# Splitting the low maxima on VectorE and moving one subtraction from TensorE to GpSimd in a sparse attention and mixture kernel

## The chip, the cores and the metric

The kernel runs on one core of one Trainium2 chip. The metric is the time of one launch in microseconds (us), the median of three runs. Five engines work side by side, each through its own list of instructions in order: TensorE (PE in the profile, its weight loads PEld), VectorE (DVE), ScalarE (ACT), GpSimd (POOL) and SyncE (SP, which here only issues transfers). An instruction that must wait for another engine holds up everything behind it on its own engine.

## The reference, cut to what matters

```python
def _attn_ref(q, k, v):                       # 8 batches, 8 heads, 576 rows, 64 columns
    scores = (1 / 8) * np.matmul(q, k.transpose(0, 1, 3, 2))
    kth = np.partition(scores, -32, axis=-1)[..., -32:-31]
    scores = np.where(scores >= kth, scores, -1000000000.0)
    ...                                       # softmax over what is left
    return np.matmul(attn, v)

def reference(...):
    x = attn_out.transpose(0, 2, 1, 3).reshape(8, 576, 512)
    return _moe_ref(x, ...)                   # 4 experts, each causal attention of 64 columns, the best 2 by gate
```

Each of the 8 x 8 x 576 rows of scores keeps its 32 largest. Then a softmax, the product with the values, and over the eight heads' results a mixture of four attention experts.

## The kernel before, in words

Two heads form a pair, so there are 32 pairs (8 batches of 4). A pair has nine tiles of 128 score rows, worked in three groups of three tiles; 96 groups in all. A pair goes through these stages:

- *Scores.* TensorE multiplies queries with keys (`scores`), ScalarE copies each tile of 128 x 576 scores from PSUM to SBUF (`copy`, L1070, tile `s`; two buffers of three tiles).
- *Top 32* (`topk`), the work of VectorE. `f1` (L1083) takes the larger and `f3` (L1086) the smaller of the two halves of 576, so 288 each, into `fa` and `fb`. `f4` is three tensor operations: A (L1090) the larger of the halves of `fa`, into `cand`; B (L1091) the smaller of them, written into `fa` itself; C (L1093) the larger of the halves of what A made, into `oct`. `low8` is three MAX8 (L1097), one for each tile, which find the eight largest of `fb`. Then `f5` (three MAX8 on B's result, L1110), and four rounds of `win` (MAX8, L1121) and `rep` (MATCH_REPLACE8, L1126). Meanwhile GpSimd does `mark` (L1102) and `low2` (L1106) on A's and C's results, `tails` (L1113) and `compare` (L1150, for the group before).
- *Stats and tail* (`stats`, `tail`). The scores are made a second time, transposed and masked (`st`), ScalarE takes the exponential (L1374, tile `pt`), and TensorE multiplies by the values `vt` into the single accumulator `acc` (`av`). The result is needed as a high part (rounded for TensorE's fast format) and the low part that the rounding left. `xh` (L1386) copies `acc` to the high part; TensorE then adds minus that high part to `acc` by a product with a negated identity (`neg`, two matmuls, 256 and 320 columns); `xl` (L1394) copies what is left. The values' buffer `vt` is single too: the load for the next pair (L968, issued from ScalarE's list) may start when `av` has read it.
- *Mixture* (`moe`), once in a batch, spread over the four pairs after it. The mixture of the last batch has no later pair to lie beside. For the last pair of all, `tail` runs in two halves (`half` is set).

GpSimd also makes low parts of the queries and keys in SBUF (`sub`, L924, two in each of 31 pairs), of the mixture's output (L1798) and of the weights (L861).

The order of every engine's list is fixed when the program is built. `Plan` takes tasks with a modelled duration, what they depend on and a priority; `order` simulates five engines and writes out the list. The table `AT` gives each task's priority by its tag; a task goes when it has the smallest number among those that could start within 150 ns of the earliest. Nothing of that simulation is used at run time, only the order that came out of it.

Of the kernel before, what the change touches and what calls it, by code (L numbers as in the profile page):

```python
# [102 lines left out]
class Plan:  # L103
# [5 lines left out]
    PORT = ("f1", "f3", "f4", "ot", "constants", "sub", "low_again")  # L109
# [32 lines left out]
    def __init__(self):  # L142
        self.tasks = []
        self.rings = set()
        self.due = 0.0
        self.at = {t: iter(x) for t, x in AT.items()}
        self.slack = 150.0

    def restart(self):
        self.tasks, self.at, self.slack = [], {}, self.SLACK  # L150
        for r in self.rings:
            r.free = [(0.0, f[1], "") for f in r.free]
# [19 lines left out]
    def order(self):  # L172
# [11 lines left out]

        def pick(e):
            free, cand = engs[e]
            feas = []
            for t, r in cand:
                s = max(free, r)
                if e == "POOL":  # L190
                    s = max(s, port["DVE"] + (0.0 if t.tag == "mark" else self.GAP))
                elif e == "DVE" and t.tag in self.PORT:
                    s = max(s, port["POOL"])
                need = {}
                for b in t.bufs:
                    if b.index is None:
                        k = need.get(b.ring, 0)
                        if k >= len(b.ring.free) or (b.ring.fifo and b.seq != b.ring.given + k):
                            break
                        need[b.ring] = k + 1  # L200
                        f = b.ring.free[k]
                        s = max(s, f[0] + self.hop(f[2], e))
                else:
                    feas.append((s, t.prio, t.n, t))
            if not feas:
                return None
            lim = min(x[0] for x in feas) + self.slack
            return min((x for x in feas if x[0] <= lim), key=lambda x: x[1:3])

        for t in self.tasks:  # L210
# [5 lines left out]
        while len(out) < len(self.tasks):  # L216
            for e in engs:
                if e in stale:
                    picks[e] = pick(e)
            best = min((x for x in picks.values() if x), key=lambda x: x[0], default=None)  # L220
# [54 lines left out]
def pool(n):  # L275
    return 2.15 * n + 165


def dma(n, rows=P):
# [8 lines left out]
PAD = {"dup1": 400.0, "dup2": 1200.0, "s10": 800.0, "s11": 300.0, "dup": 400.0, "diag": 300.0, "c7": 400.0,  # L288
# [23 lines left out]
    "again": (109, 131, 709, 670, 1023, 976, 1291, 1268, 1516, 1521, 1854, 1832, 2083, 2091, 2464, 2469, 2706, 2726,  # L312
# [7 lines left out]
    "ava": (10291,),  # L320
    "avb": (10424,),
    "avm": (2307, 2807, 3690, 4082, 4989, 5346, 6220, 6608, 7509, 7869, 8751, 9138, 9921, 10231, 10824, 10842, 10856,
        10903,),
    "c1": (2273, 2780, 3524, 3946, 4816, 5336, 6045, 6491, 7311, 7838, 8578, 9010, 9880, 10176, 10584, 10700, 10790,
        10833,),
    "c2": (2283, 2783, 3537, 3973, 4822, 5344, 6061, 6505, 7328, 7854, 8581, 9032, 9898, 10179, 10587, 10703, 10794,
        10837,),
    "c3": (2294, 2797, 3539, 3975, 4881, 5346, 6063, 6507, 7330, 7856, 8584, 9034, 9900, 10182, 10590, 10706, 10797,
        10844,),
    "c4": (2343, 2838, 3548, 3989, 4921, 5376, 6086, 6550, 7345, 7899, 8607, 9117, 9920, 10218, 10602, 10715, 10810,  # L330
        10854,),
    "c5": (2350, 2846, 3550, 4025, 4934, 5389, 6108, 6553, 7353, 7908, 8634, 9124, 9923, 10223, 10604, 10718, 10813,
        10856,),
    "c6": (2356, 2848, 3553, 4028, 4936, 5392, 6110, 6555, 7355, 7910, 8652, 9135, 9927, 10225, 10607, 10722, 10817,
        10860,),
    "c7": (2377, 2871, 3575, 4050, 4958, 5418, 6146, 6576, 7378, 7940, 8675, 9157, 9959, 10247, 10629, 10743, 10838,
        10882,),
    "cast": (38, 73, 178, 167, 405, 685, 854, 1000, 1140, 1274, 1426, 1519, 1651, 1837, 1964, 2114, 2258, 2481, 2634,
# [1632 lines left out]
```

## Time and profile before

| what | value |
|---|---|
| runs | 1138.55, 1139.99, 1141.31 us; median 1139.99 us |
| profiled execution | 1139.88 us; its span from first to last instruction 1138.1 us |
| TensorE busy | 1052.2 us, 92% of the span |
| VectorE busy | 1023.4 us, 90% |
| ScalarE busy | 931.4 us, 82% |
| GpSimd busy | 408.6 us, 36% |
| granted TensorE clock, mean | 0.971 of full |

The profiled execution is one more run, 0.11 us below the median of the three, and 1.8 us of its time lies outside its span. A busy share is an average over stages. A matmul's recorded duration overlaps that of its neighbours, so a busy TensorE is not one at its peak.

### The profile page before, as it was taken

The page shows a single profiled execution, that of the slowest core. Times are in us where ns is not written, and L with a number is a line of the kernel's source. Part 1 is how long each engine was busy: PE and PEld are TensorE (multiplying, and loading weights), DVE is VectorE, ACT ScalarE, POOL GpSimd, SP SyncE. Part 2 cuts the span into 40 slices and gives each one's busy share as a digit, 9 for nine tenths or more (in the row PEclk, how much of TensorE's full clock was granted, in tenths as well). Part 3 has the DMA queues.
Part 4 walks back from the last instruction along what each step waited for, and adds up shares of the span by engine and source line. Part 5 has one row for each costly group of instructions (what it writes and reads, how often), then busy time and mean ns, then how long its engine had stood idle before and what let it go on. Part 6 is the DMA issues. An engine that isn't in the chain of part 4 may idle for free. (4 is left out here: it accounts for less than half of the span.)

```text
span 1138.1 us, 27832 instructions
## 1 busy us (share of the span) xinstructions
PE 1052.2 (92%) x9101; PEld 882.2 (78%) x9101; DVE 1023.4 (90%) x4231; ACT 931.4 (82%) x1966; POOL 408.6 (36%) x696
## 2 busy tenths in 40 slices
PE   3378799999999999999999999999999999999996
PEld 2366578887978888887888779887887978887785
DVE  7999999999998999999999999999999999987021
ACT  5677778889878898899889898898889998888463
POOL 3443343343442434333433334332442343323101
PEclk9598989999999999999999999999999999999999
DMA  6473444444472534635554535645454535722242
GB/s 188 145 214 91 115 109 115 128 115 122 121 203 71 158 95 139 188 83 139 131 172 125 138 74 153 183 107 132 114 175 131 142 84 145 203 56 72 90 125 62
DMA packets 100123, 146.63 MB, mean 129 GB/s; under 512 B 27881, under 2 KB 39433, under 8 KB 99969
## 3 DMA queue, kind: packets, MB, share of 16 engines
q1 hardware_dynamic: 78785, 104.44, 35.1%
q10 hardware_dynamic: 21184, 40.32, 11.3%
q8 instruction: 74, 1.21, 0.5%
q14 instruction: 80, 0.66, 0.2%
HBM read 72.10 MB, written 14.31 MB: 76 GB/s over the span
## 5 line engine op out<-in xcount | busy, mean ns | idle before, releaser
L1102 POOL TENSOR_TENSOR cand<-cand 128x216 int32<-128x216 int32 x96 | 62.7, 653 | 488.5 <-DVE oct L1093 478.6
L1172 ACT ACTIVATE mask<-s,top 128x576 bf16<-128x576 f32 x288 | 213.9, 774 | 14.5 <-DVE top L1121 10.7
L715 PE MATMUL slot<-opa,opa 128*128 128x256 f32 (+4 forms) x984 | 192.6, 316 | 24.7 <-DMA opa<-raw 10.7
L715 PE MATMUL slot<-opb,opb 128*128 128x320 f32 (+1 forms) x960 | 189.7, 317 | 18.4 <-ACT s L1070 6.1
L1374 ACT ACTIVATE pt<-slot 128x576 f32<-128x576 f32 (+2 forms) x297 | 181.1, 639 | 23.3 <-PE slot L715 19.5
L1070 ACT ACTIVATE s<-slot 128x576 f32<-128x576 f32 x288 | 176.2, 651 | 27.2 <-PE slot L715 22.4
L715 PEld LDWEIGHTS slot<-opa,opa 128*128 128x128 f32 (+2 forms) x984 | 143.5, 185 | 40.7 <-ACT s L1070 16.0
L715 PE MATMUL acc<-pt,vt 128*64 128x320 f32 (+1 forms) x1280 | 171.4, 416 | 2.2 <-ACT pt L1374 2.1
L715 PEld LDWEIGHTS slot<-opb,opb 128*128 128x128 f32 x960 | 146.4, 196 | 30.4 <-ACT s L1070 8.0
L1121 DVE MAX8 top<-cand 128x8 f32<-128x160 f32 x576 | 147.6, 312 | 0.0
L715 PEld LDWEIGHTS acc<-pt,vt 128*64 128x64 f32 x1280 | 87.7, 139 | 62.5 <-issue 10.0
L1083 DVE TENSOR_TENSOR fa<-s 128x864 f32<-128x864 f32 x96 | 102.3, 1066 | 18.6 <-ACT s L1070 18.1
L715 PE MATMUL slot<-x,wt 128*128 128x288 f32 (+2 forms) x768 | 115.1, 299 | 2.1 <-ACT s L1070 1.8
L715 PE MATMUL slot<-negi,mask 128*128 128x128 bf16 (+3 forms) x1632 | 114.0, 219 | 2.1 <-ACT pt L1374 0.7
L1097 DVE MAX8 cand<-fb 128x8 f32<-128x288 f32 x288 | 112.6, 447 | 0.0
L715 PEld LDWEIGHTS slot<-x,wt 128*128 128x128 f32 x768 | 105.9, 189 | 4.6 <-ACT s L1070 2.6
L1086 DVE TENSOR_TENSOR fb<-s 128x864 f32<-128x864 f32 x96 | 102.3, 1065 | 0.0
L715 PEld LDWEIGHTS <-mask 128*128 128x128 bf16 (+1 forms) x1632 | 79.2, 102 | 24.5 <-issue 11.3
L1150 POOL TENSOR_TENSOR ind<-cand,top 128x486 bf16<-128x486 f32 x96 | 96.1, 1001 | 3.2 <-DVE top L1121 3.0
L1160 ACT ACTIVATE ind<-ind,tiny 128x486 bf16<-128x486 bf16 (+1 forms) x96 | 67.7, 705 | 29.4 <-POOL ind L1150 19.8
L1126 DVE MATCH_REPLACE8 cand<-top,cand 128x160 f32<-128x160 f32 x288 | 86.2, 310 | 0.0
L715 PE MATMUL slot<-opa,k2a 128*128 128x256 f32 (+1 forms) x320 | 70.9, 301 | 7.9 <-DMA opa<-rows 7.9
(181 smaller groups left out, 2129.8 us busy)
## 6 DMA issues: line engine op xcount, KB each, us to landing
raw<-in_qk_dram ACTq DMA_DIRECT2D x62, 288.0 KB
wt<-kept SPq DMA_DIRECT2D x68, 256.0 KB
opa<-raw SPq DMA_DIRECT2D x93, 144.0 KB
opb<-raw SPq DMA_DIRECT2D x93, 144.0 KB
vt<-in_vL_dram ACTq DMA_DIRECT2D x32, 320.0 KB
opb<-opb SPq DMA_DIRECT2D x62, 144.0 KB
opa<-opa SPq DMA_DIRECT2D x62, 144.0 KB
wt<-keptv SPq DMA_DIRECT2D x32, 260.0 KB
```

The source lines that it names most:

```text
L715: nc.tensor.matmul(o, l, r, start=start, stop=stop, skip_group_check=True)
L1070: nc.scalar.activation(s3.t[:, n], sl.t[:, o0:o0 + S], AF.Copy)
L1083: v.tensor_tensor(out=fa.t, in0=s3.t[:, :, 0:288], in1=s3.t[:, :, 288:576], op=OP.max)
L1086: v.tensor_tensor(out=fb.t, in0=s3.t[:, :, 0:288], in1=s3.t[:, :, 288:576], op=OP.min)
L1097: v.max(out=c.t[:, n, 152:160], in_=fb.t[:, n])
L1102: nc.gpsimd.tensor_tensor(out=r, in0=l, in1=r, op=OP.add)
L1121: v.max(out=w.top.t[0][:, 3 * g + n, 8 * r:8 * r + 8], in_=ones_(r, n)[:, 0:(FIRST, 72)[r]] if r < 2 else c.t[:, n, 0:160])
L1126: v.match_replace(out=(ones_(1, n), c.t[:, n, 0:72], c.t[:, n, 0:160])[r], in_values=src, imm_value=LOW, in_to_replace=w.top.t[0][:, 3 * g ...
L1150: nc.gpsimd.tensor_tensor(out=ind.t[:, 0:486].rearrange("p (a n) -> p a n", a=3), in0=c.t, in1=m32[:, 3 * g:3 * g + 3, 31:32].to_broadcast ...
L1160: nc.scalar.activation(ind.t[:, 0:n], ind.t[:, 0:n], AF.Sign, bias=tiny, accum_out=signs[:, 3 * w.p + g:3 * w.p + g + 1])
L1172: nc.scalar.activation(w.mask[j].t, s3.t[:, n], AF.Relu, bias=w.top.t[0][:, 3 * g + n, 31:32], scale=-1.0)
L1374: es[j] = add("ACT", act(a1 - a0), lambda sl=sl, pt=pt, o0=o0, a0=a0, a1=a1: nc.scalar.activation(pt.t[:, a0:a1], sl.t[:, o0 + a0:o0 + a1] ...
```

## The change

Two steps are written in another way, and the order is written out anew.

- `f4` becomes three tasks, `fa1` (A), `fa2` (B) and `fa3` (C), and `low8` three tasks of one MAX8 each. Each MAX8 depends on one of the tensor operations, so the order can lay MAX8 between A and B and between B and C. The instructions are the same, 3736 of VectorE before and after.
- For the 31 pairs that are not halved, `neg` and `xl` are gone. A second copy (`xf`) takes the whole of `acc` into the first 576 columns of the values' buffer `vt`, and GpSimd subtracts the high part from it (`xg`). The next load of `vt` must now wait for GpSimd.
- `AT` becomes a table of ranks: with it, `order` takes the tasks just as they are numbered, with no choice left to the simulation. All its numbers are new, so instructions of every engine change places. `PAD`, which `order` adds to some transfers, has new numbers too.

```diff
+        seq = sorted(self.tasks, key=lambda t: t.prio) if self.at else None
...
+            if seq:
+                t = seq[len(out)]
...
-            def f4(fa=fa, c=c, oc=oc):
+            def fa1(fa=fa, c=c, oc=oc):
+                v.tensor_tensor(out=c.t[:, :, 0:144], in0=fa.t[:, :, 0:144], in1=fa.t[:, :, 144:288], op=OP.max)
+
+            def fa2(fa=fa, c=c, oc=oc):
                 l, r = fa.t[:, :, 0:144], fa.t[:, :, 144:288]
-                v.tensor_tensor(out=c.t[:, :, 0:144], in0=l, in1=r, op=OP.max)
                 v.tensor_tensor(out=l, in0=l, in1=r, op=OP.min)
+
+            def fa3(fa=fa, c=c, oc=oc):
                 l, r = c.t[:, :, 0:72], c.t[:, :, 72:144]
                 v.tensor_tensor(out=oc.t, in0=l, in1=r, op=OP.max)
-            def low8(fb=fb, c=c):
-                for n in range(3):
-                    v.max(out=c.t[:, n, 152:160], in_=fb.t[:, n])
+            def low8(n, fb=fb, c=c):
+                v.max(out=c.t[:, n, 152:160], in_=fb.t[:, n])
...
-            t = add("DVE", 1318, f4, [t], bufs=[fa, fb, c, oc], prio=P0)
-            t8 = add("DVE", 1094, low8, [t], bufs=[fb, c], prio=P0)
+            t = add("DVE", 517, fa1, [t], bufs=[fa, fb, c, oc], prio=P0)
+            t8 = add("DVE", 365, lambda low8=low8: low8(0), [t], bufs=[fb, c], prio=P0, tag="low8")
+            t = add("DVE", 517, fa2, [t], bufs=[fa, fb, c, oc], prio=P0)
+            t8 = add("DVE", 365, lambda low8=low8: low8(1), [t, t8], bufs=[fb, c], prio=P0, tag="low8")
+            t = add("DVE", 293, fa3, [t], bufs=[fa, fb, c, oc], prio=P0)
+            t8 = add("DVE", 365, lambda low8=low8: low8(2), [t, t8], bufs=[fb, c], prio=P0, tag="low8")
...
-            a = add("PE", 0, neg, [c], bufs=[acc, xb], prio=1, kind="neg" + (half and "h"))
-            d = add("ACT", act(c1 - c0), lambda c0=c0, c1=c1, av_=av_: nc.scalar.activation(
-                xb.t[1][:, c0:c1], av_(), AF.Copy), [a], bufs=[acc, xb], prio=1, tag="xl")
+            if half:
...
+            else:
+                full = w.vt
+
+                def xf(acc=acc, full=full):
+                    nc.scalar.activation(full.t[:, 0:S], acc.t[:, 256:256 + S], AF.Copy)
+
+                def xg(full=full):
+                    nc.gpsimd.tensor_tensor(out=xb.t[1][:, 0:S], in0=full.t[:, 0:S], in1=ft(xb.t[0][:, 0:S]),
+                                            op=OP.subtract)
+                a = add("ACT", act(S), xf, [a], bufs=[acc, full], prio=1)
+                d = add("POOL", pool(S), xg, [c, a], bufs=[full, xb], prio=1)
```

What the order makes of it is seen at three places. The first is VectorE in one early group, before the change; `waits` names the engine whose progress an instruction waits for, and A is L1090, B L1091, C L1093.

```order
L1083 TENSOR_TENSOR fa_89<-s_87 128x864 [waits Activation_49]
L1086 TENSOR_TENSOR fb_90<-s_87 128x864
L1090 TENSOR_TENSOR cand_93<-fa_89 128x3x144 [waits DVE_49]
L1091 TENSOR_TENSOR fa_89<-fa_89 128x3x144 [waits DVE_49]
L1093 TENSOR_TENSOR oct_91<-cand_93 128x216
L1097 MAX cand_93<-fb_90 128x8 x3
```

The same place after the change, where A is L1103, B L1107, C L1111 and a MAX8 of `low8` is L1114.

```order
L1097 TENSOR_TENSOR fa_89<-s_87 128x864 [waits Activation_49]
L1100 TENSOR_TENSOR fb_90<-s_87 128x864
L1103 TENSOR_TENSOR cand_93<-fa_89 128x3x144 [waits DVE_49,Pool_49]
L1114 MAX cand_93<-fb_90 128x8 [waits DVE_49]
L1107 TENSOR_TENSOR fa_89<-fa_89 128x3x144 [waits DVE_49]
L1111 TENSOR_TENSOR oct_91<-cand_93 128x216
L1114 MAX cand_93<-fb_90 128x8 x2
```

One MAX8 now stands between A and B, which waits for A by VectorE's own count. This is so, or another instruction stands there, in 36 of the 96 groups; in the other 60 B still follows A directly.

The second place is ScalarE at the end of the eighth pair: before the change the high copy (L1386), the load of the next values (L968), and the low copy (L1394) after `neg`.

```order
L1386 ACTIVATE x_134<-acc_67 128x576 [waits PE_49]
L968 DMA vt_86<-in_vL_dram 128x640 [waits DMAHW6_49]
L1070 ACTIVATE s_88<-slot_64 128x576 [waits PE_49,Activation_49]
L1693 ACTIVATE ptm_4_154<-slot_65 128x512 [waits PE_49]
L1694 ACTIVATE ptm_4_154<-slot_65 64x128
L1394 ACTIVATE x_134<-acc_67 128x576 [waits PE_49]
```

After the change the whole copy (L1422) and the high copy (L1407) stand together, and the load (L982) waits for GpSimd.

```order
L1422 ACTIVATE vt_86<-acc_67 128x576 [waits DMAHW0_49,PE_49]
L1407 ACTIVATE x_134<-acc_67 128x576
L1084 ACTIVATE s_88<-slot_66 128x576 [waits PE_49,Activation_49]
L1724 ACTIVATE ptm_3_153<-slot_64 128x1024 [waits PE_49]
L1084 ACTIVATE s_88<-slot_66 128x576 [waits PE_49]
L982 DMA vt_86<-in_vL_dram 128x640 [waits DMAHW7_49,Pool_49]
L1084 ACTIVATE s_88<-slot_64 128x576 [waits PE_49]
```

The load has moved behind two score copies (L1084) and stands ahead of the third, which VectorE's next `f1` needs. In 11 of the pairs the load stands so, between a group's `mark` on GpSimd and the copies for the very next group.

The third place is GpSimd for that same pair after the change; L1119 is `mark`, L938 `sub`, L1123 `low2`, L1171 `compare` and L1425 the new subtraction.

```order
L1119 TENSOR_TENSOR cand_93<-cand_93 128x3x72 [waits DVE_49,Pool_49]
L938 TENSOR_TENSOR raw_68<-raw_68,opb_2_83 128x576 [waits DMAHW2_49,DMAHW6_49,DMAHW1_49,DMAHW7_49,DMAHW0_49,Activation_49]
L1123 TENSOR_TENSOR cand_93<-cand_93,oct_91 128x3x72 [waits Pool_49]
L1171 TENSOR_TENSOR ind_95<-cand_94,top_0_96 128x486
L1425 TENSOR_TENSOR x_134<-vt_86,x_134 128x576 [waits DMAHW0_49,Activation_49]
L1130 COPY cand_93<-cand_93 128x3x2 [waits DVE_49]
```

The subtraction comes behind four others, the first of which waits for VectorE's C. It stands nowhere in the list before.

## Rows read from the trace of the kernel before

**Rows 1.** Stretches: length; busy us (count) of PE, PEld, DVE, ACT, POOL; clock, DMA.
```profile
28.00:170.00 142.00, 104.15 (x748) 84.22 (x749) 141.24 (x616) 104.55 (x199) 57.88 (x83) 0.82 0.49 136
170.00:1048.00 878.00, 860.56 (x7633) 724.87 (x7632) 848.85 (x3514) 765.07 (x1620) 326.79 (x553) 1.00 0.48 130
1048.00:1138.00 90.00, 78.30 (x686) 64.57 (x682) 13.45 (x34) 47.56 (x128) 13.46 (x41) 0.97 0.30 92
```

**Rows 2.** VectorE's waits: who, for whom, us in total, times, longest.
```profile
DVE fa L1083 <- ACT s L1070: 18.1, 21, 4.3
DVE sm L1663 <- PE slot L715: 8.5, 9, 3.9
```

**Rows 3.** ScalarE's waits, the same view.
```profile
ACT s L1070 <- PE slot L715: 22.4, 41, 1.9
```

**Rows 4.** Timeline of VectorE in one group: start us, us, instruction, [idle before].
```profile
402.76 0.61 DVE L1090 TENSOR_TENSOR cand<-fa 128x432 f32<-128x432 f32 x1
403.40 0.61 DVE L1091 TENSOR_TENSOR fa<-fa 128x432 f32<-128x432 f32 x1
403.93 0.38 DVE L1093 TENSOR_TENSOR oct<-cand 128x216 f32<-128x216 f32 x1
404.22 1.17 DVE L1097 MAX8 cand<-fb 128x8 f32<-128x288 f32 x3
405.31 0.71 DVE L1110 MAX8 cand<-fa 128x8 f32<-128x144 f32 x3
...
410.84 1.06 DVE L1083 TENSOR_TENSOR fa<-s 128x864 f32<-128x864 f32 x1 [0.54 <-ACT s L1070]
```

**Rows 5.** Timeline of TensorE around one pair's `neg`.
```profile
1026.93 0.43 PE L715 MATMUL acc<-x,negr 128*128 128x256 f32 x2
1027.20 0.43 PE L715 MATMUL slot<-opb,opb 128*128 128x320 f32 x2
```

**Rows 6.** Groups of GpSimd: count, busy us, mean ns, idle before.
```profile
L1150 POOL TENSOR_TENSOR ind<-cand,top 128x486 bf16<-128x486 f32 x96 | 96.1, 1001 | 3.2 <-DVE top L1121 3.0
...
L1102 POOL TENSOR_TENSOR cand<-cand 128x216 int32<-128x216 int32 x96 | 62.7, 653 | 488.5 <-DVE oct L1093 478.6 <-DMA opa<-opa 6.0 <-PE slot L715 3.8
...
L1106 POOL TENSOR_TENSOR cand<-cand,oct 128x216 int32<-128x216 int32 x96 | 59.5, 620 | 5.6
...
L924 POOL TENSOR_TENSOR raw<-raw,opa 128x576 f32<-128x576 f32 x31 | 44.6, 1440 | 24.1 <-ACT opa L915 20.6 <-issue 3.3
```

**Rows 7.** VectorE's tensor operations by line: ns min/median/max, first and last start.
```profile
L1083 DVE TENSOR_TENSOR fa<-s x96: 993/1050/2010, 14.4 to 1032.4; 128x864 f32<-128x864 f32 x96
L1086 DVE TENSOR_TENSOR fb<-s x96: 1011/1051/2299, 15.4 to 1033.4; 128x864 f32<-128x864 f32 x96
L1090 DVE TENSOR_TENSOR cand<-fa x96: 592/602/1824, 16.3 to 1034.4; 128x432 f32<-128x432 f32 x96
L1091 DVE TENSOR_TENSOR fa<-fa x96: 607/608/1732, 17.0 to 1035.0; 128x432 f32<-128x432 f32 x96
L1093 DVE TENSOR_TENSOR oct<-cand x96: 370/376/1607, 17.5 to 1035.5; 128x216 f32<-128x216 f32 x96
```

**Rows 8.** Timeline of GpSimd and VectorE at the first and last lengthened operation.
```profile
23.02 1.40 POOL L924 TENSOR_TENSOR raw<-raw,opb 128x576 f32<-128x576 f32 x1
...
23.71 1.62 DVE L1083 TENSOR_TENSOR fa<-s 128x864 f32<-128x864 f32 x1
...
923.96 1.46 POOL L1798 TENSOR_TENSOR qk<-ot,qk 128x512 fp32r<-128x512 f32 x1 [5.57 <-ACT qk L1795]
924.31 1.58 DVE L1091 TENSOR_TENSOR fa<-fa 128x432 f32<-128x432 f32 x1
```

**Rows 9.** Timeline of the accumulator and the values' buffer after one pair.
```profile
857.88 0.64 ACT L1386 ACTIVATE x<-acc 128x576 fp32r<-128x576 f32 x1
860.04 0.33 ACTq L968 DMA_DIRECT2D vt<-in_vL_dram  x1
...
866.98 2.16 PE L715 MATMUL acc<-pt,vt 128*64 128x256 f32 x16
```

More of the change, by code (lines that the diff above doesn't have):

```diff
@@ L183, in ready, with first @@
             engs[t.eng][1].append((t, max([d.end + self.hop(d.by, t.eng) for d in t.deps], default=0.0)))
-        def pick(e):
[L186 to L204, printed above, removed]
+        def first(t, r):
+            e = t.eng
+            s = max(engs[e][0], r)
+            if e == "POOL":
+                s = max(s, port["DVE"] + (0.0 if t.tag == "mark" else self.GAP))
+            elif e == "DVE" and t.tag in self.PORT:
+                s = max(s, port["POOL"])
+            need = {}
+            for b in t.bufs:
+                if b.index is None:
+                    k = need.get(b.ring, 0)
+                    if k >= len(b.ring.free) or (b.ring.fifo and b.seq != b.ring.given + k):
+                        return None
+                    need[b.ring] = k + 1
+                    f = b.ring.free[k]
+                    s = max(s, f[0] + self.hop(f[2], e))
+            return s
+        def pick(e):
+            feas = [(first(t, r), t.prio, t.n, t) for t, r in engs[e][1]]
+            feas = [x for x in feas if x[0] is not None]
             if not feas:
                 return None
-            lim = min(x[0] for x in feas) + self.slack
+            lim = min(x[0] for x in feas) + self.SLACK
             return min((x for x in feas if x[0] <= lim), key=lambda x: x[1:3])
+        seq = sorted(self.tasks, key=lambda t: t.prio) if self.at else None
         for t in self.tasks:
@@ L216, in order @@
         while len(out) < len(self.tasks):
[L217 to L220, printed above, removed]
+            if seq:
+                t = seq[len(out)]
+                best = first(t, max([d.end + self.hop(d.by, t.eng) for d in t.deps], default=0.0)), t.prio, t.n, t
+            else:
+                for e in engs:
+                    if e in stale:
+                        picks[e] = pick(e)
+                best = min((x for x in picks.values() if x), key=lambda x: x[0], default=None)
             if best is None:
@@ L328 @@
[L328 to L335, printed above, removed]
@@ new lines @@
+    "cast_swap": (8, 12,),
+    "check1": (5557,),
+    "check2": (5584,),
+    "check3": (5587,),
+    "clear_bd": (5602,),
+    "compare": (87, 135, 178, 215, 270, 333, 365, 413, 469, 506, 548, 596, 651, 691, 746, 796, 849, 899, 976, 1019,
[5 rows of a table added]
+    "constants": (20,),
+    "copy": (23, 19, 25, 27, 35, 37, 75, 86, 91, 128, 132, 118, 163, 181, 172, 213, 234, 228, 293, 268, 282, 310, 338,
[15 rows of a table added]
+    "count": (94, 139, 185, 223, 284, 342, 371, 419, 479, 510, 557, 604, 659, 698, 753, 802, 855, 927, 988, 1023,
[5 rows of a table added]
@@ L1387, in tail, with neg @@
                 xb.t[0][:, c0:c1], av_(), AF.Copy), [a], bufs=[acc, xb], prio=1, tag="xh")
[L1389 to L1395 removed]
+            if half:
+                def neg(ks=ks):
+                    for k in ks:
+                        c0, c1 = halves(256)[k]
+                        mm(acc.t[:, 256 + c0:256 + c1], negr, xb.t[0][:, c0:c1], stop=True)
+                a = add("PE", 0, neg, [c], bufs=[acc, xb], prio=1, kind="neg" + (half and "h"))
+                d = add("ACT", act(c1 - c0), lambda c0=c0, c1=c1, av_=av_: nc.scalar.activation(
+                    xb.t[1][:, c0:c1], av_(), AF.Copy), [a], bufs=[acc, xb], prio=1, tag="xl")
+            else:
+                full = w.vt
[6 more added lines that the diff above has]
+                d = add("POOL", pool(S), xg, [c, a], bufs=[full, xb], prio=1)
             done.append([c, d])
```

134 lines of the change are left out of this document (62 added, 72 removed), and 589 rows, old and new, of tables (AT, BIAS).

## The prediction

> **What bounds the kernel now.** I read the stretches first [rows 1]. In the middle stretch of 878 us, which holds most of the kernel, TensorE is busy 860.6 us and VectorE 848.9 us at the full clock: they idle 17.4 and 29.2 us, 2% and 3%. Two engines share the bound, and neither can be relieved far alone. ScalarE (765 us) has 13% free, GpSimd (327 us) 63%. In the 142 us before it VectorE alone is full (141.2 us) while TensorE is at 104. In the last 90 us VectorE does 13 us of work; that is the last pair's tail and the last mixture, TensorE's.
>
> Then the waits. The largest of VectorE's waits that belongs to the repeated work is `f1` for a score copy, 18.1 us in 21 of 96 groups [rows 2]. The copy in turn waited for TensorE's scores, 22.4 us in 41 cases [rows 3]. So where VectorE idles, it is mostly because TensorE was late. The 8.5 us at L1663 lie partly in the last stretch.
>
> Last the timeline of one group [rows 4]. A starts at 402.76, B at 403.40, C at 403.93, the first MAX8 at 404.22. A and B do the same number of elements, but from A to B it is 0.64 us and from B to C 0.53. C and the MAX8 start before the end of what is ahead of them (B ends at 404.01, C starts at 403.93); B starts 0.03 after A's end. B overwrites what A reads and waits for it.
>
> **The change part by part.** *VectorE.* The instructions are the same. Where another instruction stands between A and B, A's end is past when B comes, and B follows at the spacing of its neighbours: 0.64 - 0.53 = 0.11 us saved. The order does this in 36 of 96 groups: **-4.0 us**. The bounds are nothing and 4.0, since 60 groups keep the wait. I take the whole: in [rows 4] the following instructions show no loss of their own. VectorE is full or nearly so wherever the groups lie, thus it counts in the end time.
>
> Here a page speaks against the step. The Trainium skill, VectorE: DVE Perf Modes, section "The DRAIN you can't avoid", holds that each operation is followed by an emptying of the pipe, that a semaphore costs nothing extra, and that one should lower the count of operations, not of semaphores. By it these 36 groups save nothing and the sum below would be 4.0 us higher. The trace disagrees in the 0.64 against 0.53 above.
>
> *TensorE.* `neg` goes in 31 pairs. In the timeline the pair of matmuls takes the stretch from 1026.93 to 1027.20, 0.27 us, since the next product starts behind it without a gap [rows 5]. That is 31 x 0.27 = 8.4 us of TensorE. What of it reaches the end is bounded by nothing (VectorE sets the pace) and 8.4 (each removed stretch shortens a wait of VectorE's, of which there are 18.1 us). A relief early in a pair is lost if TensorE waits for anything before the late scores, and waits come in 21 groups of 96 only. TensorE's idle 2% says that little is lost on its side, VectorE's 3% that it has little to win. I take the half: **-4.2 us**.
>
> *ScalarE.* `xl` (0.65 us) becomes `xf`, of the same shape and source; a copy of `acc` takes 0.64 [rows 9]. No difference in work. `xf` needs no `neg` ahead of it, so `acc` comes free earlier: in [rows 9] the next product of values starts 8.5 us after the first copy, so this buys nothing.
>
> *GpSimd.* 31 subtractions of 128 x 576, the same operation as `sub`, 1.44 us each [rows 6]: 44.6 us, from 36% to 40% busy. Its own idle time hides that. What does not hide is a collision with VectorE: GpSimd and an operation of VectorE with two SBUF inputs exclude each other. At 23.02 GpSimd starts a `sub` of 1.40 us; `f1`, from 23.71, takes 1.62 instead of its median 1.05. The last such case is at 924 us, B taking 1.58 instead of 0.61 [rows 7, 8]. In between the operations L1083 to L1093 are lengthened ten times in all, by 0.13 to 1.25 us, 8.6 us together over their medians; the maxima of the five lines show the size [rows 7]. All ten stand against 82 long operations of GpSimd that begin when ScalarE is ready and not when VectorE is (62 `sub`, 14 output low parts of 512 columns, 6 of the weights): 0.105 us each. The new ones are of this kind: 31 x 0.105 = **+3.3 us**. The bounds are nothing, if each falls into the MAX8 part of a group, which takes 6.4 of 10 us, and 31 x 1.25 = 39 us, if each hits; the measured share is the nearest row, and 82 operations of which ten hit speak so strongly against the upper end that the range leaves it out. A MAX8 between A and B opens a gap into which GpSimd can slip ahead of B; that is another reason not to take zero.
>
> *The values' buffer.* The reload waits for the subtraction now. In one pair the old order had the reload issued at 860.04 and the next product at 866.98, 6.9 us later [rows 9]. A subtraction of 1.44 us fits into that, so I take nothing. If that cover is gone, TensorE waits. What is queued behind the waiting reload on ScalarE is the third score copy for the next group, in 11 pairs; that is the rival below.
>
> *Order and paddings.* The paddings change no instruction. The new places of everything else can't be costed from rows; the last stretch holds the same TensorE work after the last statistics within 600 columns of moving data, counted in the two orders. Nothing is taken, and the range is widened for it.
>
> Sum: -4.0 - 4.2 + 3.3 = -4.9 us. Against the profiled execution of 1139.88 us (span 1138.1 and 1.8 outside) that is **1135.0 us**; the median of the runs is 0.1 higher, so this is 0.44% faster.
>
> **The rivals.**
>
> *TensorE is the bound.* Then its 8.4 us come off in full, and better spacing keeps collisions at the old number: -4.0 - 8.4 = 1127.5 us. For it: 98% busy in the middle stretch, and VectorE's waits lead back to TensorE [rows 1 to 3]. Against: the first 170 us are VectorE's, and a busy matmul is not one at its peak.
>
> *Nothing comes of it.* Either the wait of B is no loss that an instruction between can fill, so that VectorE's sum stays: 1139.9 - 4.2 + 3.3 = 1139.0 us. For that speaks only that it has not been seen filled. Or collisions come at over twice the old rate, because the order has less room for a GpSimd that is busier by a tenth: 1135.0 + 4 = 1139 us. For it: four of the five maxima in [rows 7] lie over a microsecond above their median, so four more cases suffice. The page cited above would give the first of these; with what the rows show I give that 0.05 and the collisions 0.14.
>
> *ScalarE stands at the reload (slower).* In 11 pairs the reload waits for a subtraction queued behind `mark`, which waits for C, and ahead of the copy that the very next `f1` needs. In the pair shown with the change this chain is C 0.38, `mark` 0.65, `sub` 1.44, `low2` 0.62, `compare` 1.00, subtraction 1.44, issue 0.33, copy 0.65: 6.5 us. From C's start to where VectorE is done with its group are 410.30 - 403.93 = 6.4 us (410.84 less the 0.54 idle) [rows 4, 6, 9]. So that one is late already, by 0.1; without a `sub`, as in the others, it is 5.1 us and some small operations. If GpSimd starts late, or `xf` is late because the product was, all of it goes to VectorE. 11 waits of 1.44 us are 15.8 us: 1150.8 us; half of it 1143. It decides from 0.65 us per pair (7.2 us in all), where the result is above 1142.2. Against: ScalarE is 13% idle and, where the copies were made earlier, nothing waits.
>
> **How the numbers follow.** My forecast, with its own range of 1130 to 1138 (the bounds of the first two terms, 4.9 less or 3 more), has 0.44; TensorE as the bound 0.18; nothing 0.19; the reload 0.19. A difference of this kernel can be told from no change from about 0.2%, that is 2.3 us: faster means below 1137.7, slower above 1142.3. Faster: 0.44 less the 0.02 of its range above 1137.7, and 0.18: 0.60. Same: 0.19 and 0.02: 0.21. Slower: 0.19. The range of 1127 to 1144 leaves out 0.06 below (more than TensorE's full relief, by the order) and half of the reload's case above, 0.10.
>
> **What would show it.** Right: the mean distance from A to the next operation falls to 0.53 in 36 groups; the matmuls on the negated identity fall from 64 to 2; `f1`'s wait for score copies falls from 18.1 to about 14 us; lengthened operations rise from ten to about thirteen; the last stretch stays at 90 us. Wrong: a large wait of ScalarE for GpSimd at the reload; TensorE waiting for the values; VectorE's sum of lengthened operations over 16 us; or a span in which neither engine's idle time moves.

## The result

The changed kernel takes 1146.88 us, median of six runs (1144.22 to 1147.76), against 1139.85 us of six runs of the kernel before on the same chip: ratio 1.0060, 95% interval 1.0046 to 1.0073. It is slower by 7 us. The forecast was 1135.0 us, faster by 5; the range of 1127 to 1144 does not hold the result.

The profiled execution took 1147.76 us, its span 1146.0. Below are the first part of its page (busy us, share of the span, instructions), its stretches with the columns of [rows 1], and VectorE's and ScalarE's waits.

```profile
PE 1048.4 (91%) x9039; PEld 873.3 (76%) x9039; DVE 1023.2 (89%) x4231; ACT 931.1 (81%) x1966; POOL 454.0 (40%) x727
```

```profile
28.00:170.00 142.00, 97.81 (x716) 77.61 (x715) 137.63 (x590) 102.47 (x193) 61.22 (x83) 0.85 0.46 128
170.00:1048.00 878.00, 854.18 (x7521) 717.51 (x7521) 842.80 (x3497) 757.55 (x1599) 364.76 (x578) 0.99 0.48 131
1048.00:1146.00 98.00, 88.37 (x766) 70.91 (x763) 22.55 (x75) 57.27 (x156) 18.03 (x49) 0.99 0.29 88
```

```profile
DVE fa L1097 <- ACT s L1084: 16.3, 18, 2.5
DVE sm L1696 <- PE slot L729: 14.3, 13, 4.5
```

```profile
ACT s L1084 <- PE slot L729: 27.5, 48, 4.7
```

TensorE has 3.8 us less work than before, VectorE as much as before (1023.2 against 1023.4 us), and both idle longer. In the middle stretch VectorE idles 35.2 us where it idled 29.2, TensorE 23.8 where it idled 17.4; in the stretch before it, where VectorE had idled 0.8 us, it now idles 4.4, and TensorE 44.2 in place of 37.9 [rows 1]. `f1` waits for score copies 16.3 us, 2 less than before, but the maxima of the mixture's scores (L1696, `sm`) wait for TensorE 14.3 us instead of 8.5 [rows 2], and the score copies wait for TensorE 27.5 instead of 22.4 [rows 3].

Cut more finely, the same columns show where.

```profile
28.00:200.00 172.00, 125.47 (x942) 103.95 (x943) 166.29 (x711) 125.89 (x239) 71.17 (x98) 0.85 0.47 128
200.00:480.00 280.00, 272.35 (x2386) 227.04 (x2383) 272.07 (x1139) 242.00 (x510) 120.42 (x193) 0.99 0.49 133
480.00:640.00 160.00, 154.90 (x1350) 129.28 (x1349) 151.50 (x618) 139.15 (x298) 66.77 (x103) 0.99 0.47 126
640.00:1040.00 400.00, 391.32 (x3486) 327.99 (x3486) 383.52 (x1606) 345.57 (x730) 166.53 (x265) 1.00 0.49 132
```

VectorE idles 5.7, 7.9, 8.5 and 16.5 us here. Before, the same four stretches had 1.7, 7.4, 3.8 and 15.6 (busy 170.33, 272.56, 156.17 and 384.38 us). The first and the third of them before:

```profile
28.00:200.00 172.00, 133.93 (x1002) 109.41 (x1003) 170.33 (x739) 129.68 (x254) 67.57 (x99) 0.85 0.48 131
480.00:640.00 160.00, 157.91 (x1396) 134.34 (x1393) 156.17 (x631) 142.80 (x307) 58.55 (x99) 1.00 0.50 134
```

Of the 10.1 us more, 4.0 arise ahead of 200 us and 4.7 between 480 and 640. About 2 us come back in the first 28 and the last 106 us, which leaves the 7.9 us by which the span grew.

The largest single wait stands in the third stretch. TensorE's timeline there, then VectorE's (start us, us, instruction, [idle before and what ended it]):

```profile
524.43 0.62 PE L729 MATMUL slot<-qk 64*128 64x256 f32 x6
524.98 0.80 PE L729 MATMUL slot<-opa,opa 128*128 128x256 f32 x4
529.25 3.55 PE L729 MATMUL acc<-pt,vt 128*64 128x256 f32 x16 [3.47 <-DMA vt<-in_vL_dram]
...
533.73 0.79 PE L729 MATMUL slot<-qk 64*128 64x384 f32 x6
```

```profile
534.62 0.96 DVE L1696 TENSOR_REDUCE sm<-slot 128x2 f32<-128x768 f32 x1 [4.50 <-PE slot L729]
```

TensorE waits 3.47 us for a load of the values that was issued too late, the mixture's scores come behind that product, and VectorE waits 4.50 us for them. This is close to one of the signs that the prediction named as wrong ("TensorE waiting for the values"), but it is one case of 31. ScalarE, which the rival saw standing at the reload, hardly stood: its score copies waited for the subtraction twice, 1.1 us together.

```profile
ACT s L1084 <- POOL x L1425: 1.1, 2, 0.6
```

### The profile page after: what moved, and what is told of

Read it like the earlier page. It is cut to its first block, busy times and chain, and to the rows that moved or that the text cites. A ratio compares the mean times of both kernels' runs of the same rounds, so it can differ in the third digit from the quotient of the medians.

```text
span 1146.0 us, 27739 instructions
## 1 busy us (share of the span) xinstructions
PE 1048.4 (91%) x9039; PEld 873.3 (76%) x9039; DVE 1023.2 (89%) x4231; ACT 931.1 (81%) x1966; POOL 454.0 (40%) x727
## 5 line engine op out<-in xcount | busy, mean ns | idle before, releaser
L1119 POOL TENSOR_TENSOR cand<-cand 128x216 int32<-128x216 int32 x96 | 62.5, 651 | 425.9 <-DVE oct L1111 415.8
L1084 ACT ACTIVATE s<-slot 128x576 f32<-128x576 f32 x288 | 177.9, 652 | 39.5 <-PE slot L729 27.5
L729 PEld LDWEIGHTS slot<-opb,opb 128*128 128x128 f32 x960 | 143.6, 194 | 27.4 <-ACT s L1084 10.9
L1097 DVE TENSOR_TENSOR fa<-s 128x864 f32<-128x864 f32 x96 | 102.2, 1065 | 16.8 <-ACT s L1084 16.3
L1114 DVE MAX8 cand<-fb 128x8 f32<-128x288 f32 x288 | 117.0, 450 | 0.0
L1100 DVE TENSOR_TENSOR fb<-s 128x864 f32<-128x864 f32 x96 | 105.0, 1093 | 0.0
L1171 POOL TENSOR_TENSOR ind<-cand,top 128x486 bf16<-128x486 f32 x96 | 96.1, 1001 | 1.2 <-DVE stat L1238 1.2
L729 PE MATMUL slot<-opa,k2a 128*128 128x256 f32 (+2 forms) x320 | 70.3, 299 | 6.4 <-DMA opa<-rows 6.4
```

Source lines behind the costliest of these rows:

```text
L729: nc.tensor.matmul(o, l, r, start=start, stop=stop, skip_group_check=True)
L1084: nc.scalar.activation(s3.t[:, n], sl.t[:, o0:o0 + S], AF.Copy)
L1097: v.tensor_tensor(out=fa.t, in0=s3.t[:, :, 0:288], in1=s3.t[:, :, 288:576], op=OP.max)
L1100: v.tensor_tensor(out=fb.t, in0=s3.t[:, :, 0:288], in1=s3.t[:, :, 288:576], op=OP.min)
L1114: v.max(out=c.t[:, n, 152:160], in_=fb.t[:, n])
L1119: nc.gpsimd.tensor_tensor(out=r, in0=l, in1=r, op=OP.add)
```

## The experiments

Two theories stood at the start. *O*: the new order costs the time, and the edits are worth about what was forecast. *G*: the GpSimd subtraction and the reload tied to it cost it. To part them, each order was run with each edit. A kernel takes its order from the table of ranks, so the order of before was written as such a table too, with the same instructions in the same places (in e1's trace the lists of ScalarE and GpSimd are those of before, one by one). Every kernel below differs from that one, or from the changed kernel, only in what is named. Differences in us are the ratio's, times the median of before.

| run | order | split | subtraction | median us | ratio to before (95%) |
|---|---|---|---|---|---|
| before | old | no | no | 1139 to 1140 | 1 |
| e1 | old | 96 groups | no | 1141.13 | 1.0016 (1.0001 to 1.0031) |
| e2 | old | no | 31 pairs, reload tied | 1156.36 | 1.0152 (1.0134 to 1.0170) |
| e5 | old | no | 24 pairs, not tied | 1142.57 | 1.0029 (1.0018 to 1.0041) |
| e11 | old | no | 18 pairs, not tied | 1142.09 | 1.0023 (1.0010 to 1.0037) |
| e6 | old | 96 groups | 24 pairs, not tied | 1145.11 | 1.0046 (1.0029 to 1.0063) |
| e3 | new | no | no | 1152.62 | 1.0119 (1.0102 to 1.0136) |
| e4 | new | as changed | no | 1153.83 | 1.0121 (1.0102 to 1.0139) |
| e9 | new | no | 31 pairs | 1145.61 | 1.0059 (1.0039 to 1.0079) |
| changed | new | as changed | 31 pairs | 1146.88 | 1.0060 (1.0046 to 1.0073) |
| e10 | new | as changed | 24 pairs, loads early | 1146.55 | 1.0067 (1.0040 to 1.0095) |
| e7 | old (new behind 1108 us) | 96 groups | 31 pairs, reload tied | 1160.99 | 1.0186 (1.0153 to 1.0218) |
| e8 | new to 200 us, then old | no | no | 1141.69 | 1.0022 (1.0007 to 1.0037) |
| e12 | new to 600 us, then old | no | no | 1148.28 | 1.0084 (1.0067 to 1.0101) |
| e13 | new, 480 to 600 us old | no | no | 1157.12 | 1.0142 (1.0120 to 1.0164) |
| e14 | old, 480 to 600 us new | no | no | 1146.17 | 1.0061 (1.0044 to 1.0078) |

**e1, the split alone.** The order of each group:

```diff
-f4  low8
+fa1 low8(0) fa2 fa3  low8(1) low8(2)
```

> The order of before in every place, with one edit: in all 96 groups one MAX8 of low8 stands between A and B, the other two behind C; neg and xl stay. Theory O (the new order costs the time, the edits themselves are worth about what was forecast): 96 separations at 0.11 us are 10.6 us less of VectorE's work, of which the wait for f1 and for TensorE may take some back, so 1130 to 1137 us, and the spacing from A to the next instruction 0.52 us in all 96 groups. Theory G (the GpSimd subtraction and the reload behind it cost the time): the same, 1130 to 1137 us. A theory that the split itself hurts: no faster than before (1138 us or more).

No gain: 1141.13 us lies outside what both theories expected, and the part of *O* that gave the edits about the worth that was forecast falls with it. The split does what it was to do. VectorE's timeline of one group, with A at L1114, a MAX8 at L1125, B at L1118, C at L1122:

```profile
403.09 0.60 DVE L1114 TENSOR_TENSOR cand<-fa 128x432 f32<-128x432 f32 x1
403.61 0.45 DVE L1125 MAX8 cand<-fb 128x8 f32<-128x288 f32 x1
403.98 0.59 DVE L1118 TENSOR_TENSOR fa<-fa 128x432 f32<-128x432 f32 x1
404.49 0.38 DVE L1122 TENSOR_TENSOR oct<-cand 128x216 f32<-128x216 f32 x1
```

From A to the next instruction it is 0.52 us, and the MAX8 and B lose nothing for it. But in the middle stretch of e1 and among its waits:

```profile
170.00:1048.00 878.00, 857.32 (x7609) 723.82 (x7611) 840.07 (x3512) 761.28 (x1613) 326.71 (x554) 1.00 0.47 130
```

```profile
DVE fa L1108 <- ACT s L1095: 25.0, 27, 4.3
```

VectorE is busy 8.8 us less than before in that stretch, with 3512 instructions against 3514 [rows 1]: what was saved has become idle time. `f1`'s wait for score copies alone has grown by 6.9 us over the run (25.0 against 18.1 [rows 2]).

**e2, the subtraction alone**, with the changed kernel's code in the old order: `xf` behind `xh`, the load some 3.5 us of modelled time behind `xh`.

> The order of before in every place, with the other edit: in 31 pairs neg and xl are gone, xf stands directly behind xh on ScalarE, the subtraction on GpSimd where the modelled time puts it (about 1.4 us behind xh), and the load of the next values some 3.5 us of modelled time behind xh. f4 is one task as before. Theory O: 1135 to 1141 us (31 times 0.27 us of TensorE given back, some of it used, some lost to collisions of the subtraction with VectorE's tensor operations). Theory G: 1144 us or more, with waits of TensorE for the values or of ScalarE for GpSimd that together make at least 6 us.

G seemed to hold: 17 us slower, with TensorE waiting for values three times.

```profile
PE acc L720 <- DMA vt<-in_vL_dram: 8.4, 3, 5.1
```

The load's place was mine, though, so e2 says only that a tied reload can cost this much.

**e3 and e4, the new order without the edits.** In e3 both edits are out, in e4 only the subtraction. `neg` stands 0.65 us of modelled time behind `xh`, `xl` 1.2 us or later.

```diff
-xh  xf  xg(GpSimd)
+xh  neg(TensorE)  xl
```

> The order of the changed kernel with both edits taken out: in each group A, B, C stand ahead of the three MAX8 (in the places that the six had), and neg and xl are back in 31 pairs, neg 0.65 us of modelled time behind xh and xl behind it; the load of the next values stays where the changed order has it. Theory O: 1146 us or more, up to 1155, since the edits' gains are gone and the order's loss stays. Theory G: back to 1138 to 1142 us.

> The changed kernel with neg and xl put back in the 31 pairs (neg 0.65 us of modelled time behind xh, xl behind it), the split of f4 and low8 as the changed kernel has it. Theory O: 1146 to 1152 us, as slow as the changed kernel or slower by the 8.4 us of neg that come back in part. Theory G: 1134 to 1140 us, the loss gone with the subtraction.

Theory G falls: with the subtraction gone the new order is not back at 1140 us but at 1153 (e4 even 1.8 us above what *O* expected). Some of the 13.6 us is my placing of `neg` (TensorE waits for the high copy 3.8 us in e3 and 2.6 in e4, before 0.6). Putting `neg` back costs some 7 us in either pair of runs (e4 against changed, e3 against e9), of which this placing may be up to 3, so the subtraction is a gain in the order that was written for it. The split is worth nothing there (e4 against e3; e9 below); in e3 and e9 it is undone in 27 of its 36 groups, since in nine another instruction of VectorE's stands between A and B.

**e5 and e6, the subtraction without the reload.** `xf` writes into an exponential tile that is free until the next pair's last one. Seven pairs, whose high copy comes late, keep `neg`.

```diff
-full = w.vt
+full = ptb[8]
```

> The order of before in every place, f4 as one task. In 24 of the 31 pairs neg and xl are replaced by xf and the GpSimd subtraction, but xf writes its whole copy into one of the nine exponential tiles pt instead of into the values' buffer, so the load of the next values stays at its old place and waits for nothing new; the seven pairs whose high copy comes late (the second of each batch from the second batch on) keep neg and xl. Theory T (TensorE sets the time from some 170 us on, and e2 lost it by its reload): 24 times 0.27 us are 6.5 us less of TensorE's work, most of it seen, 1132 to 1136 us. Rival C (the subtraction itself costs, by lengthened operations of VectorE and one more step before the high and low parts are ready): 1139 us or more.

> As e5, with the split of e1 in all 96 groups as well. Theory T: VectorE's 10 us become useful only where TensorE no longer holds the end, so as e5 or up to 4 us faster, 1128 to 1136 us. Rival C: 1139 us or more.

Theory T falls too. The stretch of e5 and its waits:

```profile
170.00:1048.00 878.00, 851.23 (x7554) 714.96 (x7556) 851.04 (x3520) 761.76 (x1612) 356.04 (x572) 1.00 0.48 130
```

```profile
PE slot L1249 <- ACT stat L1246: 17.2, 11, 8.7
```

TensorE is busy 9.3 us less than before in the middle stretch and idles that much longer [rows 1]; over the whole run its wait for the statistics that VectorE and ScalarE make has grown from 10.8 to 17.2 us. Before it was:

```profile
PE slot L1245 <- ACT stat L1242: 10.8, 6, 8.6
```

`f1`'s wait falls by 2.2 us (15.9 against 18.1 [rows 2]), but VectorE is busy 2.2 us longer in the stretch: six of the 24 subtractions lengthened operations of VectorE's, by 6.2 us (a seventh by 0.2). In e6 both engines have less work, and the time is no shorter than with either edit alone.

**e11, the subtraction without its collisions.** As e5, with `neg` back in the six pairs that collided.

> As e5 (order of before, whole copy into a pt tile), but neg and xl are back also in those six pairs whose GpSimd subtraction fell on a tensor operation of VectorE there and lengthened it, 6.2 us in all; 18 subtractions are left. Theory C (e5's loss of 2.9 us is these collisions, and TensorE's saving is real): 18 times 0.27 us are 4.9 us less of TensorE's work and few lengthened operations, 1135 to 1139 us. Theory W (what is freed turns into waits, whatever is freed): 1139 to 1142 us.

None of the 18 subtractions left lengthens a tensor operation of VectorE's by over 0.26 us, and the time hardly changes: 1142.09 us. `f1` waits 20.8 us in this run. So the collisions are not what keeps e5 from a gain; theory W, that what is freed turns into a wait, came within 0.1 us.

**e9, the changed kernel without its split** (the six places of a group in the order A, B, C, MAX8, MAX8, MAX8).

> The changed kernel with the split alone undone: in each group the six places of A, B, C and the three MAX8 are taken by A, B, C, MAX8, MAX8, MAX8 in this order; order, subtraction and reload as changed. It is the last of the four corners in the new order (e3 without edits 1152.6, e4 with the split 1153.8, the changed kernel with both 1146.9 us). If the split's 4 us of VectorE's work lie on the path: 1149 to 1152 us. If VectorE's gain is waited away, as e1, e4 and e6 show it: 1145 to 1148 us.

1145.61 us, the same as with the split within the intervals; 27 of the 36 separations are gone in it.

**e10, the changed kernel with seven loads untied.** The seven pairs keep `neg`, and their load stands where `xf` stood.

```diff
-if half:
+if half or w.p in (5, 9, 13, 17, 21, 25, 29):
```

> The changed kernel, but in the seven pairs whose high copy comes late (the second of each batch from the second batch on) neg and xl are back, so the load of the next values needs no subtraction, and it stands where the whole copy stood, directly behind the product. In the changed kernel one of these loads came late: TensorE waited 3.5 us for it at 529 us, and VectorE 4.5 us for TensorE at 534 us. Theory R (the tied reload costs what these two waits show): 1141 to 1144 us, less than 1 us of wait for values, and the step of VectorE's lost time at 529 us gone. Theory O (the loss is the new order's, in many small waits): 1145 to 1149 us, the seven neg (1.9 us) given back besides.

TensorE waits for no values in this kernel, and the time is the same (1146.55 us, with a wide interval). At the same place two other waits stand now, one for statistics and one for the same scores:

```profile
525.21 0.46 DVE L1266 TENSOR_REDUCE stat<-stat 128x9 f32<-128x288 f32 x1 [1.70 <-ACT stat L1262]
533.03 0.96 DVE L1709 TENSOR_REDUCE sm<-slot 128x2 f32<-128x768 f32 x1 [1.47 <-PE slot L742]
```

So the late load is only the last of several things that make VectorE wait there, and without it most of the wait stays.

**e7, e8 and e12, orders joined in time.** Up to a modelled time the steps of one order, then all that is left in the other.

```diff
-old order
+new order up to 200 us (e8) or 600 us (e12), then the old one
```

> The changed kernel with the order of its first 200 us of modelled time taken from the order of before (there with the split in the form of e1 and the subtraction as in e2), and the changed order for all that is left. Theory E (the loss lies in the stretch up to 200 us, where the changed order leaves TensorE idle 9.6 us longer, which it can't make up later because it is busy without a pause from there on): 1136 to 1140 us. Rival L (the later part of the new order costs as much or more): 1144 us or more.

> The counterpart of e7 without edits: the first 200 us of modelled time in the order of e3 (the changed order with both edits taken out), and the order of before for all that is left. In e3 TensorE was idle 4.3 us longer between 28 and 170 us than before. Theory E: 1143 to 1150 us, most of the 13.6 us that e3 lost. Rival L: 1138 to 1141 us.

> As e8, with the order of e3 for the first 600 us of modelled time and the order of before for the rest, no edits. e3 was 8 to 10 us behind before at 600 us, of which half came in one step between 518 and 562 us; e8 was 4 us behind at 200 us and 4 us at the end. Theory O (the loss of the new order is a loss of the stretches in which it arises, and isn't made up later): 1146 to 1150 us. A theory that the late part of the order makes it: 1139 to 1143 us.

Theory E was wrong: of the 13.6 us, the first 200 us of the new order carry 2.5 (e8, just above what rival L expected), though TensorE idles there longer. By 600 us it is 9.6 (e12). e7 is not the kernel that its expectation describes. Its trace has ScalarE's list of e2, instruction by instruction, and VectorE's of e1, up to some 1108 us; the new order follows only there. So it tests neither theory, but it is a corner that was missing: the old order with both edits and the tied reload, 1160.99 us, slower than the changed kernel by 14.

**e13 and e14, one stretch.** Steps of 480 to 600 us exchanged in e3, and in the old order.

> e3 (new order, no edits) with the steps that it has between 480 and 600 us of modelled time (about 495 to 620 us of the trace) put in the order in which the kernel before has them. Theory L (the step of some 5 us between 518 and 562 us is made there, by where the products with the values and the mixture's scores stand in TensorE's list, and is not made up later): 1146 to 1149 us, against 1152.6 us for e3. Theory B (TensorE was already behind when it came there and would hand the loss on anywhere): 1151 to 1154 us.

> The counterpart: the order of before everywhere, but the steps between 480 and 600 us of modelled time in the order of e3, no edits. Theory L: 1143 to 1146 us. Theory B: 1138.5 to 1141 us, since TensorE is not behind there in the old order.

e14 is 7.0 us slower than before (theory L, 0.2 us above its range). Its profiled execution is 4.1 us slower, and the stretches show that it loses them in that place:

```profile
28.00:200.00 172.00, 133.40 (x1009) 108.09 (x1010) 171.11 (x745) 129.79 (x254) 67.05 (x99) 0.85 0.48 131
200.00:480.00 280.00, 273.54 (x2414) 229.87 (x2413) 273.53 (x1143) 243.47 (x509) 108.80 (x183) 0.99 0.50 135
480.00:640.00 160.00, 154.93 (x1343) 130.71 (x1344) 149.32 (x615) 137.32 (x291) 59.07 (x98) 0.99 0.48 129
640.00:1040.00 400.00, 391.12 (x3515) 330.21 (x3513) 383.12 (x1582) 346.69 (x733) 146.89 (x248) 1.00 0.48 130
```

From 480 to 640 us VectorE idles 10.7 us (before: 3.8), TensorE 5.1 (before: 2.1); in the other three stretches neither is idle over 1.4 us longer than before. No edit is in this kernel, TensorE did not come there late (the last `neg` ahead of the place starts at 514.99 us, before at 517.28), and the new order of 120 us costs as much as the whole change. What it looks like, on TensorE and on VectorE:

```profile
516.81 0.53 PE L740 MATMUL slot<-qk,negr 128*128 128x288 f32 x2 [1.28 <-ACT qk L1636]
...
517.40 0.44 PE L740 MATMUL slot<-qk 64*128 64x128 f32 x4
518.44 0.33 PE L740 MATMUL slot<-qk 64*128 64x128 f32 x2 [0.61 <-ACT qk L1643]
...
519.91 1.33 PE L740 MATMUL slot<-opa,opa 128*128 128x256 f32 x4
521.17 2.65 PE L740 MATMUL acc<-pt,vt 128*64 128x256 f32 x16
...
524.75 0.79 PE L740 MATMUL slot<-qk 64*128 64x384 f32 x6
```

```profile
516.08 0.76 DVE L1810 TENSOR_TENSOR ot<-slot,sm 128x576 f32<-128x576 f32 x1 [0.63 <-DMA sm<-gates]
517.88 0.46 DVE L1264 TENSOR_REDUCE stat<-stat 128x9 f32<-128x288 f32 x1 [1.04 <-ACT stat L1260]
525.65 0.96 DVE L1695 TENSOR_REDUCE sm<-slot 128x2 f32<-128x768 f32 x1 [1.42 <-PE slot L740]
```

The mixture's product on `negr` (for the low parts of its queries and keys) stands directly ahead of the first scores that need its result (517.40), so TensorE waits for a copy of ScalarE's ahead of it, 1.28 us, and for another behind it, 0.61 us. In the kernel before the product stands at 513.06 us and those scores at 517.87, with other matmuls in between, and neither waits. Then matmuls of the next scores (519.91) stand ahead of the product with the values, and VectorE, whose list has the mixture's maximum at a fixed place, waits. These are five waits of 0.6 to 1.4 us within ten microseconds; there are more of this size to 640 us.

The place can be followed through all kernels by two starts of `f1`, the 49th and the 50th. The stretches between them, in the columns of [rows 1], one line each for before, changed, e3, e14 and e13:

```profile
518.12:531.12 13.00, 12.42 (x105) 8.42 (x103) 12.78 (x47) 10.68 (x33) 5.03 (x8) 1.00 0.53 142
522.15:539.88 17.73, 13.97 (x109) 8.92 (x107) 13.23 (x48) 11.88 (x35) 4.99 (x8) 0.90 0.61 157
520.42:538.47 18.05, 16.14 (x111) 10.08 (x109) 13.52 (x49) 12.96 (x37) 4.74 (x8) 0.81 0.58 149
514.40:530.91 16.51, 14.59 (x113) 9.66 (x111) 13.43 (x48) 12.96 (x37) 4.75 (x8) 0.90 0.52 141
526.98:539.97 12.99, 12.41 (x105) 8.40 (x103) 12.77 (x47) 10.68 (x33) 5.02 (x8) 1.00 0.56 163
```

VectorE idles 0.2 us here before and 4.5 in the changed kernel. It idles 3.1 to 4.5 in all seven kernels that have the new order at this place (changed, e3, e4, e9, e10, e12, e14), and 0.2 to 0.8 in seven that have the old one (before, e1, e5, e6, e8, e11, e13). Six of the seven have no join near it, and e13, with old steps between new ones, does not lose here. (In e2 and e7 VectorE idles 6 us: old order, but TensorE waits there for the tied load.) A second place, from the 82nd `f1` to the 83rd, is like it; the lines are before and the changed kernel:

```profile
876.28:887.96 11.68, 11.68 (x93) 9.55 (x89) 11.60 (x46) 10.93 (x26) 4.82 (x11) 1.00 0.44 124
883.50:898.34 14.84, 14.53 (x116) 11.80 (x116) 12.56 (x48) 13.89 (x31) 7.09 (x12) 1.00 0.47 117
```

VectorE idles 2.2 to 2.4 us in the six kernels with the new order there (changed, e3, e4, e9, e10, e13), 0.1 to 0.7 in the others.

The first place has one thing more. TensorE's granted clock is 1.00 there in the seven kernels with the old order (1.00 is 2.4 GHz, 0.50 is 1.2). In all seven with the new order it falls to 0.50, just behind TensorE's waits or during them, for 3.4 us (6.8 in e3 and e4). The first two lines are such stretches of the changed kernel and of e3, the third a product of e3 inside its own:

```profile
528.70:532.10 3.40, 2.85 (x14) 1.49 (x16) 1.43 (x12) 0.00 (x0) 1.40 (x3) 0.50 0.66 180
524.50:531.30 6.80, 6.80 (x30) 3.68 (x30) 5.78 (x21) 3.77 (x13) 2.75 (x5) 0.50 0.92 239
527.27 4.11 PE L740 MATMUL acc<-pt,vt 128*64 128x256 f32 x16
```

These 16 matmuls took 2.16 us at 1.00 [rows 9]. So part of what the place costs is the slower clock behind the waits and not the waits themselves; no run parts the two.

e13, the mirror image, came out at 1157 us, outside both expectations. It loses elsewhere, about its second join and behind it: from the 57th to the 73rd `f1` it falls behind the kernel before by 6.2 us more, and the clock is at 0.50 there twice, for 3.4 us each. Why is not shown.

## Why the prediction was wrong

**The step that failed is "Order and paddings", where "nothing is taken".** It said that the new places of everything else can't be costed from rows, and left them at zero with a wider range. The old order had idle times of 2% and 3% on two engines, and that was read as "two engines share the bound". It also means that nearly every step was in a place where it waits for nothing, so moving thousands of steps could hardly gain and could easily lose. The runs show loss there with no edit in the kernel: 13.6 us in e3 (part of it `neg`'s place), 9.6 when the new order ends at 600 us (e12), 7.0 for 120 us of it (e14). In the profiled execution of the changed kernel VectorE idles 8.1 us longer than before, and the two places above, which the new order makes whatever the edits, hold 6.5 of them. The range went 4 us above no change; it should have gone over ten.

**A sum of separate terms could not come out.** The order and the edits do not add up. Without the edits the new order costs 13.6 us. With both of them the old order is no better than the new: 1160.99 us with the reload tied (e7), and 1145.11 with 24 subtractions and free loads (e6), whose interval overlaps that of the changed kernel. So even in the old order, where this term is nothing, the edits cost 5 to 21 us where 4.9 were to be gained. The prediction's own range hid this: with its first two terms at nothing the sum is 1139.9 + 3.3 = 1143.2 us and not 1138, and its rivals let only one term fail at a time. The rival "TensorE is the bound" falls with e5, where TensorE has 9.3 us less to do in the middle stretch and the end comes no sooner.

**The split, -4.0.** The size was right on VectorE: 0.52 us from A to the next instruction in the 36 groups, 0.64 in the 60 others. In one of the 36, with A at L1103 and a MAX8 at L1114:

```profile
408.63 0.60 DVE L1103 TENSOR_TENSOR cand<-fa 128x432 f32<-128x432 f32 x1
409.14 0.45 DVE L1114 MAX8 cand<-fb 128x8 f32<-128x288 f32 x1
```

What failed is "thus it counts in the end time". 96 such groups gained nothing (e1, and e6 against e5), nor did 27 of the 36 (e9). The rule that the prediction cites here from the Trainium skill (VectorE: DVE Perf Modes, "The DRAIN you can't avoid"), that a semaphore costs nothing extra, does not fit the spacing, 0.52 us against 0.64; the sum by it, nothing for this term, is what the times show, for another reason.

**The negated product, -4.2.** Half of 8.4 us was a mean of two cases. In the new order some 7 us come back with it (e3 against e9, e4 against the changed kernel; up to 3 of them are the placing of `neg`), in the old one none (e5, e11). TensorE's busy share does not tell which holds. That it hangs on whether the other engines' lists are laid so that something waits for the freed time is my reading; no run isolates it.

**The collisions, +3.3.** The ten lengthened operations at the five lines of [rows 7] stayed ten, and 8.6 us. But the new subtractions hit six times, for 5.7 us together: twice at those lines, and four times at a line that I had not counted, the first operation of the statistics (L1238, 128 x 9). In the timeline of one case:

```profile
425.04 1.41 POOL L1425 TENSOR_TENSOR x<-vt,x 128x576 fp32r<-128x576 f32 x1
425.26 1.23 DVE L1238 TENSOR_TENSOR stat<-top 128x9 f32<-128x9 f32 x1
```

Its median is 0.17 us. The cases of this line that are lengthened by over 0.1 us go from four and 1.5 us before to eight and 5.6, so the net is +4.1 where 3.3 was taken. This is about what the 36 separations save (36 times 0.12), and VectorE's busy time did not fall.

**ScalarE and the reload, nothing taken.** ScalarE held: 931.1 us against 931.4. The reload was late once; untying seven loads, that one among them, gains nothing that can be measured (e10, with a wide interval). The rival "ScalarE stands at the reload" has the right sign and, at 1143 to 1151 us, the right size, but not the mechanism: ScalarE's copies waited 1.1 us there, not 7 to 16.

**The other signs.** 64 matmuls on the negated identity and `acc` went to 2. `f1`'s wait fell to 16.3, not to 14. The tail held: from the last L1238 at 1054.3 us to the end it is 91.7 us, before it was 92.9 (from 1045.2 to 1138.1).

**What stays open.** Why less work on both engines (e6) ends later in the old order; and how much of the loss is TensorE's clock. Its granted mean is 0.965 over the six runs of the changed kernel (0.962 to 0.970) and 0.971 over 77 runs of the kernel before (0.966 to 0.976); 0.006 of 1146 us would be 7 us of TensorE's time at full clock, an estimate from these means. The clock alone does not order the kernels: e5 has 0.973 and e14 0.970, and both are slower than before. No kernel here beats the one before. e1, with the least loss, is 1.0016.

## What to carry to other kernels

Where every engine's list is fixed and two engines are over 95% busy, an engine's freed time can turn into its own wait: here, in the old order, 8 us off VectorE's busy time (e1), 6 and 9 off TensorE's (e11, e5) and both (e6) gave nothing. Judge such a change by its corners, the edit in the old order, the new order without the edit, and both, before believing a gain of either; here they did not add up. To find where an order loses, lay the starts of one repeated instruction (here `f1`) of two kernels side by side: the places stand out as steps. When a table moves everything, a prediction should give the order its own term: count the places where a product now stands directly ahead of its consumer, price each at a wait of about a microsecond, and look at the granted clock behind it.

## What the runs showed of the hardware

An operation of VectorE with two inputs in SBUF that starts under a GpSimd subtraction waits for its end, however small it is: 9 columns, 0.17 us by themselves, took 1.23 and ended 0.04 us behind the subtraction above. Larger ones end later: in the traces of before and changed 0.24 us behind it with 216 columns, 0.46 with 432 and 0.92 with 864, where they take 0.38, 0.61 and 1.05 alone. The Trainium skill, SBUF — State Buffer, section "SBUF: two separate sides", says that the port pair is an exclusive lock for the whole instruction and that the loser blocks fully; this trace agrees, with 1.23 against 0.17 us. A collision's price is therefore what is left of GpSimd's instruction, less some 0.14 us in all these cases, and not a matter of VectorE's operation.
